# The last two matrix products of a fused attention and SoLU kernel: from a planner's order to an order written out by hand

## The chip, the cores and the metric

The kernel runs on one core of one Trainium2 chip. The metric is the time of one execution on the device in microseconds, and lower is better. A profile of one execution shows five engines: PE (TensorE; PEld is its weight loads), DVE (VectorE), ACT (ScalarE), POOL (GpSimd) and SP (SyncE), whose queue issues nearly all DMA transfers.

## The reference, cut to what matters

Three layers follow each other; the change touches the third only.

```python
def _moe2_ref(x, w_in, w_out, g_ln):          # x: 1792 x 768
    h = x @ w_in                               # 768 x 1024
    h_max = np.max(h, axis=-1, keepdims=True)
    e = np.exp(h - h_max)
    sm = e / (np.sum(e, axis=-1, keepdims=True) + 1e-09)
    solu = h * sm
    mu = np.mean(solu, axis=-1, keepdims=True)
    var = np.mean((solu - mu) ** 2, axis=-1, keepdims=True)
    ln = (solu - mu) / np.sqrt(var + 1e-06) * g_ln
    return (ln @ w_out)                        # 1024 x 768
```

In front of it stand softcapped attention (4 x 12 heads, 448 x 64) and a layer `((x @ w1) * (x @ w2)) @ w3 @ w_out`. The kernel folds `w3 @ w_out @ w_in` into one 1024 x 1024 matrix beforehand, so that `h` is the product of the gated rows `ab` (1792 x 1024) with that matrix.

## The kernel before, in words

**Stages.** Attention (with the folding of weights beside it) and the gated products fill the first 569 us; the change leaves their operations alone. Then come the two stages that it rewrites. Stage 3 computes `h = ab @ folded` and SoLU with the normalisation; stage 4 computes `ln @ w_out` with `g_ln` folded into the weights. Each goes over 7 pairs of 128-row tiles, so there are 14 **rounds**: 0 to 6 in stage 3, 7 to 13 in stage 4.

**One round** is a Strassen-Winograd scheme, function `seven`: seven products named by number, in the order 1, 2, 6, 7, 5, 4, 3, where the plain scheme has eight. A product is 12 matmuls with 512 result columns in stage 3 and 384 in stage 4: four blocks of the inner dimension, times three, since each fp32 operand is split into a high part (a cast to fp32r, ACT, L176) and a low part (a subtraction, DVE, L177). Operands 1, 2 and 4 are quarters of the two tiles; 6, 7, 5 and 3 are sums of quarters (`s1` to `s4`, DVE). Results lie in PSUM banks `u` (two buffers, three products added into one), `y` and `v`. Three are copied out by ACT (L775, the terms p1, u2, p7), three are added to such a copy by DVE (L782, L791, L794), and the last `u` is copied by ACT (L796). A product that adds into `u` or `v` waits for the copy of what stood there.

**SoLU** (`solu`, L824 to L834) of a tile: greatest value of each row (DVE), exp with row sums (ACT), product with `h` (DVE), mean, squares (ACT), variance (DVE, then POOL to the power -1/2), normalisation (DVE), store to a DRAM buffer `c_dr`.

**Stage 4's operands** come back from `c_dr` in 32 x 32 blocks (`load_c`, L865: four DMAs of 128 KB for a tile, in pieces of 128 bytes), are transposed by DVE into PSUM (L839), and split as before. Its weight blocks `wg` (seven, 768 KB each) take the places of stage 3's blocks `ws`: loaded in halves (L518) once the last product with the old block is done, then split by ACT and DVE (L176, L177). Of `ws`, the blocks 4 and 3 (`LATE`) can only be loaded and split during round 0, since their places belong to earlier stages.

**Order.** Nothing in stages 3 and 4 is ordered by hand: a planner that simulates the program's time (`schedule_with_timeline_sim=True`) puts the traced instructions of each engine in order. It may start a product of one round before the products of the round before are done. On the chip each engine then works through its own list in order and waits on semaphores.

Of the kernel before, what the change touches and what calls it, by code (L numbers as in the profile page):

```python
# [9 lines left out]
F32 = mybir.dt.float32  # L10
# [8 lines left out]
P = 128  # L19
# [80 lines left out]
def attention_moe_solu(ctx: ExitStack, tc: tile.TileContext, q, k, v, cap, w12, w3t, wo, win, wout2, g_ln, out):  # L100
# [225 lines left out]
    fw, pos, place, held = {}, [0], {}, {}  # L326
    res = [opened(left, "resa")]
# [43 lines left out]
    def fold():  # L371
# [33 lines left out]
        close(left, 3)  # L405
# [48 lines left out]
    def plan_x(b, parts=range(NPAIR // 2)):  # L454
        for part in parts:
# [6 lines left out]
            def load(i=i, pairs=pairs):  # L462
                rb[i] = conv.tile([P, 2, S], F32, tag="rb", name=f"rb{i}")
# [72 lines left out]
    def plan_last(f):  # L536
        for u in range(2):
            i = len(ahead.items)

            def rest(i=i, u=u):  # L540
                t = conv.tile([P, DM // 2], F32, tag="wg", bufs=2, name=f"wg{f}_{u}")
# [30 lines left out]
    def load_ab(n):  # L572
        for t in (2 * n, 2 * n + 1):
            landing(f"ab{t}", ab_dr[:, :, t * P:(t + 1) * P].rearrange("f p t -> p f t"), NF * P, F32)

    def operand(a, m, x, name, p=None):
        a[m] = op.tile([P, 2, HALF], F32R, tag="op", bufs=NOP, name=f"{name}_{m}") if p is None else p
        split(a[m][:, 0], a[m][:, 1], x)
# [3 lines left out]
    def first_operands():  # L582
        x1, x2 = lands["ab0"], lands["ab1"]
# [3 lines left out]
        def begin(m, x):  # L587
            operand(begun, m, x, "a0", w3p.tile([P, 2, HALF], F32R, tag="w3", bufs=W3, name=f"a0_{m}"))
# [5 lines left out]
    ahead.add("a0", lambda: load_ab(0), lambda: None, first_operands, None, lambda: (NF + 2, PASSES[1][0]) in fin)  # L594
# [168 lines left out]
    NTT = NT // P  # L763
    PAIRS = NTT // 2

    def seven(n, a, wb, w, c1, c2, other):

        def product(bank, m, first):
            for k in range(NF // 2):
                for i, (x, e) in enumerate(THREE):  # L770
                    pe.matmul(bank, a[m][:, x, k * P:(k + 1) * P], wb[m][:, e, k, :], start=(first and k == 0 and i == 0), stop=(k == NF // 2 - 1 and i == 2), skip_group_check=not first)  # L771

        def kept(bank, name):
            t = hp.tile([P, HALF], F32, tag="kept", bufs=2, name=f"{name}_{n}")[:, :w]
            act.copy(t, bank)  # L775
            return t

        u, y, v = (ps.tile([P, HALF], F32, tag=g, bufs=2 if g == "u" else 1, name=f"{g}_{n}")[:, :w] for g in ("u", "y", "v"))
        product(u, 1, True)
        p1 = kept(u, "p1")  # L780
        product(y, 2, True)
        dve.tensor_tensor(c1[:, :w], y, p1, ALU.add)  # L782
        other(0)
        product(u, 6, False)
        u2 = kept(u, "u2")
        other(1)
        product(v, 7, True)
        p7 = kept(v, "p7")
        other(2)
        product(u, 5, False)  # L790
        dve.tensor_tensor(c2[:, w:], u, p7, ALU.add)  # L791
        other(3)
        product(v, 4, False)
        dve.tensor_tensor(c2[:, :w], v, u2, ALU.add)  # L794
        product(u, 3, False)
        act.copy(c1[:, w:], u)  # L796

    def operands(n):

        x1, x2 = (lands.pop(f"ab{t}") for t in (2 * n, 2 * n + 1))  # L800
        a11, a12, a21, a22 = x1[:, :HALF], x1[:, HALF:], x2[:, :HALF], x2[:, HALF:]
        s3, s4 = (hp.tile([P, HALF], F32, tag="sm", bufs=4, name=f"s{i}_{n}") for i in (3, 4))
        a, name = (dict(begun) if n == 0 else {}), f"a{n}"
        if n:
            s1, s2 = (hp.tile([P, HALF], F32, tag="sm", bufs=4, name=f"s{i}_{n}") for i in (1, 2))
            operand(a, 1, a11, name)
            operand(a, 2, a12, name)
            dve.tensor_tensor(s1, a21, a22, ALU.add)
            dve.tensor_tensor(s2, s1, a11, ALU.subtract)
            operand(a, 6, s2, name)  # L810
        else:
            s1, s2 = a.pop("sums")
        dve.tensor_tensor(s3, a11, a21, ALU.subtract)
        operand(a, 7, s3, name)
        operand(a, 5, s1, name)
        operand(a, 4, a22, name)
        dve.tensor_tensor(s4, a12, s2, ALU.subtract)
        operand(a, 3, s4, name)
        return a

    def solu(t, h):
        st = hp.tile([P, 16], F32, tag="st", bufs=3, name=f"st{t}")
        e = hp.tile([P, DF], F32, tag="e", bufs=2, name=f"e{t}")
        dve.tensor_reduce(st[:, 0:1], h, axis=AX.X, op=ALU.max, negate=True)  # L824
        act.activation(e, h, AF.Exp, bias=st[:, 0:1], accum_out=st[:, 1:2])  # L825
        dve.tensor_scalar(st[:, 1:2], st[:, 1:2], 1e-9, None, ALU.add)
        dve.reciprocal(st[:, 2:3], st[:, 1:2])
        dve.scalar_tensor_tensor(e, e, st[:, 2:3], h, ALU.mult, ALU.mult, accum_out=st[:, 3:4])  # L828
        dve.tensor_scalar(st[:, 4:5], st[:, 3:4], -1.0 / DF, None, ALU.mult)
        act.activation(h, e, AF.Square, bias=st[:, 4:5], accum_out=st[:, 5:6])  # L830
        dve.tensor_scalar(st[:, 6:7], st[:, 5:6], 1.0 / DF, 1e-6, ALU.mult, ALU.add)
        pool.tensor_tensor(st[:, 7:8], st[:, 6:7], neghalf, ALU.pow)
        dve.tensor_scalar(e, e, st[:, 4:5], st[:, 7:8], ALU.add, ALU.mult)
        sync.dma_start(out=c_dr[t], in_=e)  # L834

    def turned(n, tps, q):

        tps[q] = ps.tile([P, HALF], F32, tag="tp", bufs=4, name=f"tp{n}_{q}")
        dve.transpose(tps[q], lands[f"c{2 * n + q % 2}"][:, q // 2 * HALF:(q // 2 + 1) * HALF])  # L839

    def turned_operands(n, tps):
        a11, a21, a12, a22 = (tps[q] for q in range(4))
        s1, s2, s3, s4 = (hp.tile([P, HALF], F32, tag="sm", bufs=4, name=f"cs{i}_{n}") for i in range(4))
        a, name = {}, f"c{n}"
        operand(a, 1, a11, name)
        operand(a, 2, a12, name)
        x21 = conv.tile([P, HALF], U32, tag="cv", bufs=2, name=f"x21_{n}").bitcast(F32)
        act.copy(x21, a21)
        dve.tensor_tensor(s1, a22, x21, ALU.add)
        dve.tensor_tensor(s2, s1, a11, ALU.subtract)  # L850
        operand(a, 6, s2, name)
        dve.tensor_tensor(s3, a11, x21, ALU.subtract)
        operand(a, 7, s3, name)
        operand(a, 5, s1, name)
        operand(a, 4, a22, name)
        dve.tensor_tensor(s4, a12, s2, ALU.subtract)
        operand(a, 3, s4, name)
        return a

    def load_c(n):  # L860
        for t in (2 * n, 2 * n + 1):
            lands[f"c{t}"] = conv.tile([P, 2 * HALF], U32, tag="ld", bufs=LANDS, name=f"ldc{t}").bitcast(F32)
            blocks = c_dr[t].rearrange("(i a) (k g b) -> g a k i b", i=P // SQ, g=P // SQ, b=SQ)
            for g in range(P // SQ):
                sync.dma_start(out=lands[f"c{t}"][g * SQ:(g + 1) * SQ].rearrange("p (k i b) -> p k i b", k=NF, b=SQ), in_=blocks[g])  # L865

    w, wg = DM // 2, {}

    def load_wg(m):
        wg[m] = (wsp if m in EARLY[:4] else place["w5"] if m in EARLY else wsl).tile([P, 2, NF // 2, HALF], F32R, tag=f"w{m}", name=f"wg{m}")[:, :, :, :w]  # L870
        for part in range(2):
            block_load(m, part, G4, tg_dr, wg[m])
        for part in range(2):
            block_split(wg[m], part)

    for m in LATE:
        for part in range(2):
            block_load(m, part, W4, tw_dr, ws[m])
    load_ab(1)
    a = operands(0)  # L880
    for m in LATE:
        for part in range(2):
            block_split(ws[m], part)
    for n in range(PAIRS):
        tps, last = {}, n + 1 == PAIRS
        if last:
            load_c(0)
# [82 lines left out]
```

## Time and profile before

| | us |
|---|---|
| median of 3 runs (822.79 to 824.30) | 823.5 |
| the profiled execution | 821.78 |
| its span on the core | 820.0 |
| PE busy | 802.0 (98%) |
| DVE busy | 603.8 (74%) |
| ACT busy | 477.9 (58%) |

A busy share is a mean over all stages. PE time counts a matmul until its modelled end, so a busy PE can still be a slow one: the granted clock beside it tells whether it ran at its upper (1.00) or lower (0.50) level. The profile numbers the kernel's lines; a line of a helper (L176, L177) serves many places, and the tile names tell them apart.

### The profile page before, as it was taken

Reading aid. Unit: us, or ns where it says so; the run is one execution under the profiler, and the core shown is the slowest. Engines: PE = TensorE matmul, PEld = TensorE weight load, DVE = VectorE, ACT = ScalarE, POOL = GpSimd, SP = SyncE. Lnnn points to the kernel's source line nnn. Section 1 sums busy time; section 2 is a strip of 40 time slices with the busy share of each in tenths; the row PEclk is TensorE's granted clock in tenths of the full one; section 3 lists DMA queues with packets and bytes.
Section 4 is the critical chain, followed back from the end, with each engine's and each line's share of the span. In section 5 each row is a group of like instructions: output and inputs, shape, how many; then the busy total and the mean of one; then the engine's idle time right before and its main releaser. Section 6 shows DMA issues by size and latency. Waiting matters only on the chain. (4 is left out here: it accounts for less than half of the span.)

```text
span 820.0 us, 12057 instructions
## 1 busy us (share of the span) xinstructions
PE 802.0 (98%) x4251; PEld 674.0 (82%) x4251; DVE 603.8 (74%) x1076; ACT 477.9 (58%) x739; POOL 74.8 (9%) x147
## 2 busy tenths in 40 slices
PE   8999999999999999999989999999999999889998
PEld 4657888876777888888869999999888888789997
DVE  5989968788776687789756653332988879999851
ACT  6767868787677777667753311112556555765431
POOL 1110110110311211101111000000000000000000
PEclk9999999999999999999999999999999999889999
DMA  7878645678886345779656999981533349858411
GB/s 232 273 265 271 207 162 147 184 228 269 284 274 221 118 133 199 242 261 298 189 172 185 294 373 399 328 259 57 189 114 118 102 103 215 234 143 185 110 40 77
DMA packets 151292, 167.18 MB, mean 204 GB/s; under 512 B 71232, under 2 KB 124224, under 8 KB 149696
## 3 DMA queue, kind: packets, MB, share of 16 engines
q1 hardware_dynamic: 146240, 155.22, 59.2%
q0 software_dynamic: 4992, 11.19, 5.1%
q8 instruction: 33, 0.54, 0.3%
q14 instruction: 27, 0.22, 0.1%
HBM read 113.25 MB, written 47.53 MB: 196 GB/s over the span
## 5 line engine op out<-in xcount | busy, mean ns | idle before, releaser
L610 PE MATMUL ab<-xs,wt 128*128 128x448 f32 x1152 | 236.8, 362 | 0.4 <-ACT x L308 0.4
L610 PEld LDWEIGHTS ab<-xs,wt 128*128 128x128 f32 x1152 | 215.9, 188 | 17.1 <-ACT x L308 0.8
L259 ACT ACTIVATE sc<-sc,qscale 128x896 f32<-128x896 f32 (+1 forms) x96 | 84.9, 885 | 35.2 <-PE sc L251 26.5
L260 ACT ACTIVATE p<-sc,capt 128x896 f32<-128x896 f32 (+1 forms) x96 | 85.6, 917 | 1.4
L292 PE MATMUL o<-hi,v 128*66 128x448 f32 (+1 forms) x360 | 85.0, 371 | 1.3 <-ACT x L308 1.2
L381 PEld LDWEIGHTS f<-w,w_o 128*128 128x128 f32 x576 | 72.0, 189 | 10.1 <-issue 5.7
L771 PE MATMUL u<-ws,a 128*128 128x512 f32 x336 | 79.6, 390 | 0.0
L381 PE MATMUL f<-w,w_o 128*128 128x256 f32 x576 | 77.7, 287 | 0.9 <-DVE w_o L177 0.9
L275 DVE TENSOR_TENSOR lo<-p,hi 128x896 fp32r<-128x896 f32 x60 | 65.0, 1085 | 13.9 <-ACT hi L271 13.7
L771 PEld LDWEIGHTS u<-ws,a 128*128 128x128 f32 x336 | 63.0, 188 | 13.1
L399 PE MATMUL f<-w_i,w 128*128 128x512 f32 x288 | 70.2, 393 | 1.3 <-ACT w L176 1.0
L771 PE MATMUL u<-wg,c 128*128 128x384 f32 x336 | 64.3, 341 | 3.9 <-ACT h L796 3.9
L399 PEld LDWEIGHTS f<-w_i,w 128*128 128x128 f32 x288 | 53.7, 188 | 14.7 <-ACT w L176 1.4
L771 PEld LDWEIGHTS u<-wg,c 128*128 128x128 f32 x336 | 60.3, 193 | 4.5 <-ACT h L796 4.3
L614 ACT COPY a<-ab 128x448 f32<-128x448 f32 x32 | 17.0, 532 | 77.8 <-PE ab L610 71.9
L292 PEld LDWEIGHTS o<-hi,v 128*66 128x66 f32 (+1 forms) x360 | 39.1, 135 | 26.8 <-issue 8.5
L271 ACT CAST hi<-p 128x896 fp32r<-128x896 f32 x60 | 56.6, 947 | 0.3
L618 DVE TENSOR_TENSOR abs<-ab,a 128x448 f32<-128x448 f32 x32 | 19.9, 620 | 44.7 <-PE ab L610 28.7
L171 DVE SCALAR_TENSOR_TENSOR cv<-ld,cv 128x512 uint32<-128x512 uint32 (+1 forms) x80 | 52.0, 658 | 0.6
L172 DVE SCALAR_TENSOR_TENSOR cv<-ld,cv 128x512 uint32<-128x512 uint32 (+1 forms) x80 | 52.0, 658 | 0.5
L170 DVE TENSOR_SCALAR cv<-ld 128x512 uint32<-128x512 uint32 (+1 forms) x80 | 32.6, 411 | 20.5 <-DMA ld<-in_w 8.5
L309 POOL DMA_DIRECT2D xr<-x x48 | 25.4, 533 | 198.0 <-ACT x L308 190.9
(129 smaller groups left out, 1246.9 us busy)
## 6 DMA issues: line engine op xcount, KB each, us to landing
ld<-in_w SPq DMA_DIRECT2D x24, 512.0 KB, 4.9
w_dr<-wt SPq DMA_DIRECT2D x6, 1536.0 KB, 6.9
wt<-w_dr SPq DMA_DIRECT2D x6, 1536.0 KB, 8.1
ld<-in_w3t SPq DMA_DIRECT2D x16, 512.0 KB, 4.2
ab_dr<-abs SPq DMA_DIRECT2D x32, 224.0 KB, 5.0
ldab<-ab_dr SPq DMA_DIRECT2D x14, 512.0 KB, 3.9
c_dr<-e SPq DMA_DIRECT2D x14, 512.0 KB, 3.5
ldc<-c_dr SPq DMA_DIRECT2D x56, 128.0 KB, 3.3
```

Source lines behind the costliest of these rows:

```text
L170: dve.tensor_scalar(x, hi, 5, 2, ALU.logical_shift_left, ALU.logical_shift_right)
L171: dve.scalar_tensor_tensor(x, hi, 0xC0000000, x, ALU.bitwise_and, ALU.bitwise_or)
L172: dve.scalar_tensor_tensor(x, lo, 29, x, ALU.logical_shift_right, ALU.bitwise_or)
L259: act.activation(sc[:, :w, :S], sc[:, :w, :S], AF.Tanh, scale=qscale)
L260: exp_[n, c] = act.activation(p, sc[:, :w, :S], AF.Exp, scale=capt)
L271: act.copy(hi, p)
L275: dve.tensor_tensor(lo, p, raw(hi), ALU.subtract)
L292: product_.append(pe.matmul(outs[n, j][:v_.shape[-1], :S], v_, t[rows, j if c < 3 else 0], **flags))
L381: pe.matmul(f[:, :QW], lw[:, a], rw[:, e], start=(g == 0 and m == 0), stop=(g == NF - 1 and m == 2))
L399: pe.matmul(f, w34[:, a, c, :], rw[:, e], start=(c == 0 and m == 0), stop=(c == NC - 1 and m == 2))
L610: pe.matmul(pp[f, b, i][:, :S], w[:, u], xs[b, c][:, e], start=(c == 0 and m == 0), stop=(c == NC - 1 and m == 2))
L771: pe.matmul(bank, a[m][:, x, k * P:(k + 1) * P], wb[m][:, e, k, :], start=(first and k == 0 and i == 0), stop=(k == NF // 2 - 1 and i == 2 ...
```

## The change

All of stages 3 and 4 is traced in a `manual_schedule` block: each engine runs its instructions in the order in which they are written. The order is a table of slots `(round, product)`. In each slot the product is issued, then the entries planned for that slot, then the copy or addition that takes its result out of PSUM.

- **Order of products**: strictly 1, 2, 6, 7, 5, 4, 3 in each round.
- **Operands**: the cast of an operand stands a slot (mostly) ahead of its subtraction. Operands 1 and 2 are cast and subtracted in one instruction each (1024 wide), likewise 6 and 7. The two transposes of 512 columns become one of 1024.
- **Maxima**: the three additions that leave PSUM in stage 3 become `tensor_tensor_reduce` with a running maximum, the last copy becomes a DVE `tensor_scalar` with a maximum (ACT keeps it in round 6 and in stage 4); the two row-maximum reductions of a pair go, and two negations of a column come.
- **Normalisation** moves from DVE to ACT (`Identity` with scale and bias), with one more POOL instruction for the bias.
- **Weights of stage 4**: each block is one DMA and one split instead of two, with the cast two or more slots after the load is written.
- **A fourth landing**: tiles read back land in four buffers in turn, not three; `rb` and `wg` of the earlier stages get a pool of their own, `early`, that is free in the last two stages. Operand and sum tiles are laid out anew.
- **SoLU of round 6** runs in rounds 9 to 11; before, it was traced in round 7.

```diff
-NOP = 9
+ORDER = EARLY + LATE
+LEAST = -3.0e38
...
+    early = opened(left, "early")
...
+    def product(r, j):
+        m, w = ORDER[j], HALF if r < PAIRS else DM // 2
...
+    def added(r, i, half, g, keep):
+        w = banks[g].shape[-1]
+        dst = h[r][i][:, half * w:(half + 1) * w]
+        if r >= PAIRS:
+            dve.tensor_tensor(dst, banks[g], keeps[keep], ALU.add)
+            return
+        first = (i, half) in ((0, 0), (1, 1))
+        dve.tensor_tensor_reduce(dst, banks[g], keeps[keep], 1.0, LEAST if first else col(r, MAX, i), ALU.add, ALU.max, col(r, MAX if first else MOST, i))
...
+            if r < LAST:
+                dve.tensor_scalar(dst, banks["u"], 0.0, col(r, MAX, 0), ALU.add, ALU.max, accum_out=col(r, MOST, 0))
+            else:
+                act.copy(dst, banks["u"])
...
-        dve.tensor_reduce(st[:, 0:1], h, axis=AX.X, op=ALU.max, negate=True)
+        dve.tensor_scalar(col(r, NEG, i), col(r, MOST, i), -1.0, None, ALU.mult)
...
-        dve.tensor_scalar(e, e, st[:, 4:5], st[:, 7:8], ALU.add, ALU.mult)
+        act.activation(h[r][i], es[r, i], AF.Identity, bias=col(r, SHIFT, i), scale=col(r, RSTD, i))
...
+    def landed():
+        k = taken[0]
+        taken[0] += 1
+        if k % 4 < LANDS:
+            return conv.tile([P, 2 * HALF], U32, tag="ld", bufs=LANDS, name=f"ldx{k}").bitcast(F32)
+        return op.tile([P, 2 * HALF], F32, tag="lx", name=f"ldx{k}")
...
+    plan(0, 0, (load_late, 4), (load_late, 3), (load, 1, 0), (load, 1, 1), (begun_sums,))
+    plan(0, 1, (high, 0, 7))
+    plan(0, 2, (high, 0, 5), (low, 0, 7), (high_w, ws, 4, 0))
+    plan(0, 3, (high, 0, 4), (sum4, 0), (low, 0, 5), (low_w, ws, 4, 0), (high_w, ws, 4, 1))
+    plan(0, 4, (high, 0, 3), (low, 0, 4), (low_w, ws, 4, 1), (high_w, ws, 3, 0), (high_w, ws, 3, 1))
+    plan(0, 5, (low, 0, 3), (low_w, ws, 3, 0), (low_w, ws, 3, 1))
...
+    plan(LAST, 0, (load, A + 1, 0))
+    for m, s in zip(ORDER, range(len(ORDER))):
+        plan(LAST + (s + 1) // 7, (s + 1) % 7, (load_wg, m))
+        if m == 7:
+            plan(LAST, 4, (load, A + 1, 1))
+    for n, s in ((2, 1), (3, 7), (4, 13), (5, 19)):
+        plan(A + s // 7, s % 7, (load, A + n, 0), (load, A + n, 1))
...
+    for m, s, t in ((1, 3, 4), (2, 4, 5), (6, 5, 6), (7, 6, 7), (5, 8, 9), (4, 9, 10), (3, 10, 11)):
+        plan(LAST + s // 7, s % 7, (high_w, wg, m))
+        plan(LAST + t // 7, t % 7, (low_w, wg, m))
...
+    for n in range(PAIRS - 1):
+        plan(A + n + 1, 0, (give, A + n, 1))
+        plan(A + n + 1, 1, (give, A + n, 0))
+    with tc.manual_schedule():
+        for r in range(2 * PAIRS):
+            for j in range(len(ORDER)):
+                product(r, j)
+                for todo in side.pop((r, j), ()):
+                    todo()
+                evict(r, j)
+        for i in (1, 0):
+            give(2 * PAIRS - 1, i)
```

Here `LAST` is 6 and `A` is 7; `high` is a cast on ACT, `low` its subtraction on DVE, `high_w` and `low_w` the same for a weight block, `give` the store of a result tile. The other rounds are planned in the same way: in stage 3 the operands of round n are made from slot -7 to slot 2 counted from its start, in stage 4 from slot -6 to slot 4; the SoLU of round r runs through the slots of round r + 1 (exp in slots 0 and 1, squares in 2 and 3, normalisation in 4 and 5).

## Rows read from the trace of the kernel before

**Rows 1.** Windows: us; busy PE, PEld, DVE, ACT, POOL; granted clock; DMA share; GB/s.

```profile
645.41:664.45 19.04, 19.04 (x85) 15.77 (x85) 15.56 (x30) 10.77 (x19) 1.51 (x3) 1.00 0.43 116
683.49:709.40 25.91, 25.91 (x122) 22.13 (x121) 25.46 (x44) 18.09 (x32) 1.10 (x2) 1.00 0.97 243
709.40:727.83 18.43, 12.04 (x49) 11.71 (x49) 18.43 (x32) 11.72 (x20) 1.10 (x2) 0.75 0.67 168
```

**Rows 2.** Timeline of PE, and of all engines at the end: start, us, instruction, idle.

```profile
569.25 2.96 PE L771 MATMUL u<-ws,a 128*128 128x512 f32 x12
...
629.37 5.60 PE L771 MATMUL u<-ws,a 128*128 128x512 f32 x24
634.81 2.88 PE L771 MATMUL v<-ws,a 128*128 128x512 f32 x12
...
713.35 4.21 PE L771 MATMUL u<-wg,c 128*128 128x384 f32 x12 [3.94 <-ACT h L796]
...
724.74 3.61 PE L771 MATMUL y<-wg,c 128*128 128x384 f32 x12 [2.45 <-DVE o L782]
...
736.83 4.32 PE L771 MATMUL u<-wg,c 128*128 128x384 f32 x24
740.99 1.55 PE L771 MATMUL y<-wg,c 128*128 128x384 f32 x8
...
816.07 0.48 ACT L796 COPY o<-u 128x384 f32<-128x384 f32 x1 [5.76 <-PE u L771]
```

**Rows 3.** Timeline of the SP queue and of ACT where the stages meet.

```profile
682.44 6.65 SPq L865 DMA_DIRECT2D ldc<-c_dr  x7
...
701.33 5.00 SPq L865 DMA_DIRECT2D ldc<-c_dr  x5
...
708.39 2.10 SPq L518 DMA_DIRECT2D wg<-tg_dr  x2
...
710.59 0.83 ACT L176 CAST wg<-wg 128x768 fp32r<-128x768 f32 x1 [3.17 <-DMA wg<-tg_dr]
...
712.72 0.58 ACT L796 COPY h<-u 128x512 f32<-128x512 f32 x1
```

**Rows 4.** Groups by line and shape, 600 to 820 us: busy us, mean ns.

```profile
L177 DVE TENSOR_TENSOR c<-cs,c 128x512 fp32r<-128x512 f32 x28 | 18.8, 683 | 4.5 <-ACT c L176 4.1
L828 DVE SCALAR_TENSOR_TENSOR e<-e,st,h 128x1024 f32<-128x1024 f32 x14 | 17.8, 1278 | 0.0
L176 ACT CAST c<-cs 128x512 fp32r<-128x512 f32 x28 | 17.0, 622 | 8.9 <-PE u L771 8.1 <-PE v L771 0.8
L825 ACT ACTIVATE e<-h,st 128x1024 f32<-128x1024 f32 x13 | 15.0, 1153 | 7.4 <-DMA c_dr<-e 3.4 <-issue 3.2 <-DVE st L824 0.8
L824 DVE TENSOR_REDUCE st<-h 128x1 f32<-128x1024 f32 x12 | 14.1, 1208 | 1.9 <-ACT h L796 1.9
L177 DVE TENSOR_TENSOR wg<-wg 128x768 fp32r<-128x768 f32 x14 | 13.2, 946 | 0.5 <-ACT wg L176 0.5
L176 ACT CAST wg<-wg 128x768 fp32r<-128x768 f32 x14 | 11.5, 835 | 9.7 <-DMA wg<-tg_dr 5.0 <-DMA wg<-wg_dr 4.6
L833 DVE TENSOR_SCALAR e<-e,st 128x1024 f32<-128x1024 f32 x14 | 11.2, 802 | 2.0 <-POOL st L832 1.9
L791 DVE TENSOR_TENSOR h<-u,p 128x512 f32<-128x512 f32 x6 | 4.1, 685 | 0.2 <-PE u L771 0.2
```

**Rows 5.** DMA issues, whole execution: count, KB each, median us to landing.

```profile
ldc<-c_dr SPq DMA_DIRECT2D x56, 128.0 KB, 3.3
out<-o SPq DMA_DIRECT2D x14, 384.0 KB, 2.3
ws<-w_dr SPq DMA_DIRECT2D x6, 512.0 KB, 8.9
wg<-tg_dr SPq DMA_DIRECT2D x8, 384.0 KB, 5.7
```

**Rows 6.** Timeline of DVE in round 0: two subtractions end to end.

```profile
577.06 1.29 DVE L177 TENSOR_TENSOR a<-s,a 128x512 fp32r<-128x512 f32 x2
```

More of the change, by code (lines that the diff above doesn't have):

```diff
@@ L570, in attention_moe_solu, with gated_tile, load_first @@
         plan_block(EARLY[4], part)
[L572 to L578, printed above, removed]
+    def gated_tile(t):
+        return ab_dr[:, :, t * P:(t + 1) * P].rearrange("f p t -> p f t")
+    def load_first():
+        for t in range(2):
+            landing(f"x{t}", gated_tile(t), NF * P, F32)
     begun = {}
     def first_operands():
-        x1, x2 = lands["ab0"], lands["ab1"]
+        x1, x2 = lands["x0"], lands["x1"]
         s1, s2 = first_sums = [conv.tile([P, HALF], U32, tag="cv", bufs=2, name=f"s{i}_0").bitcast(F32) for i in (1, 2)]
@@ L762, in attention_moe_solu @@
     ps = ps_cm.__enter__()
[L763 to L796, printed above, removed]
@@ L836, in turned @@
[L836 to L858, printed above, removed]
@@ L860, in load_c @@
[L860 to L874, printed above, removed]
@@ L876, in attention_moe_solu @@
-    for m in LATE:
+    PAIRS = NT // P // 2
+    LAST = PAIRS - 1
+    wg, banks, keeps, h, a, x, sums, es, sts = {}, {}, {}, {}, {0: begun}, {0: (lands.pop("x0"), lands.pop("x1"))}, {0: {}}, {}, {}
+    MAX, MOST, NEG, SUM, INV, TOTAL, MEAN, SQUARES, VAR, RSTD, SHIFT = range(0, 22, 2)
+    side, both, taken = {}, {}, [2]
+    def product(r, j):
+        m, w = ORDER[j], HALF if r < PAIRS else DM // 2
+        g, first = {1: "u", 2: "y", 6: "u", 7: "v", 5: "u", 4: "v", 3: "u"}[m], m in (1, 2, 7)
+        if first:
+            banks[g] = ps.tile([P, HALF], F32, tag=g, bufs=2 if g == "u" else 1, name=f"{g}_{r}")[:, :w]
+        b = ws if r < PAIRS else wg
+        for k in range(NF // 2):
+            for i, (p, e) in enumerate(THREE):
+                pe.matmul(banks[g], a[r][m][:, p, k * P:(k + 1) * P], b[m][:, e, k, :], start=(first and k == 0 and i == 0), stop=(k == NF // 2 - 1 and i == 2), skip_group_check=not first)
@@ new lines, in store, with load @@
+    def store(r, i):
+        sync.dma_start(out=c_dr[2 * r + i], in_=h[r][i])
+    def landed():
[4 more added lines that the diff above has]
+        return op.tile([P, 2 * HALF], F32, tag="lx", name=f"ldx{k}")
+    def load(r, i):
+        x.setdefault(r, {})[i] = t = landed()
+        if r < PAIRS:
+            sync.dma_start(out=t.rearrange("p (f t) -> p f t", t=P), in_=gated_tile(2 * r + i))
+            return
+        blocks = c_dr[2 * (r - PAIRS) + i].rearrange("(i a) (k g b) -> g a k i b", i=P // SQ, g=P // SQ, b=SQ)
+        for g in range(P // SQ):
+            sync.dma_start(out=t[g * SQ:(g + 1) * SQ].rearrange("p (k i b) -> p k i b", k=NF, b=SQ), in_=blocks[g])
@@ new lines, in high @@
+    def high(r, m):
+        if m in (1, 6, 7):
+            t = op.tile([P, 2, 2, HALF], F32R, tag="two", bufs=3, name=f"a{r}_{m}")
+            if m != 7:
+                a.setdefault(r, {}).update({m: t[:, 0], m + 1: t[:, 1]})
+                both[r, m] = t[:, :, 0], t[:, :, 1]
+            else:
+                a[r][m] = t[:, 1]
+                both[r, m] = t[:, 1, 0], t[:, 1, 1]
+        else:
+            a[r][m] = t = op.tile([P, 2, HALF], F32R, tag="one", bufs=3, name=f"a{r}_{m}")
+            both[r, m] = t[:, 0], t[:, 1]
+        act.copy(both[r, m][0], source(r, m))
@@ new lines, in parts, with high_w, low_w, plan @@
+    def parts(t, part):
+        return (t[:, i, rows(part), :] for i in range(2))
+    def high_w(t, m, part=None):
+        hi, lo = parts(t[m], part)
+        act.copy(hi, raw(lo))
+    def low_w(t, m, part=None):
+        hi, lo = parts(t[m], part)
+        dve.tensor_tensor(lo, raw(lo), raw(hi), ALU.subtract)
+    def plan(r, j, *entries):
+        for f, *args in entries:
+            side.setdefault((r, j), []).append(lambda f=f, args=args: f(*args))
+    A = PAIRS
+    STEPS = ((turn, 0), (turn, 1), (high, 1), (low, 1), (copy21,), (sum1,), (sum2,), (sum3,), (high, 6), (low, 6), (high, 5), (low, 5), (high, 4), (low, 4), (sum4,), (high, 3), (low, 3))
@@ new lines, in attention_moe_solu, with give @@
+    plan(A + 2, 2, (greatest, LAST), (negate, LAST, 0), (negate, LAST, 1))
+    for i in range(2):
+        plan(A + 2, 3 + i, (exponential, LAST, i))
+        plan(A + 3 + i, 0, (weigh, LAST, i))
+        plan(A + 3 + i, 1, (squares, LAST, i))
+        plan(A + 3 + i, 3, (spread, LAST, i))
+        plan(A + 3 + i, 4, (normal, LAST, i))
+        plan(A + 3 + i, 5, (store, LAST, i))
+    def give(r, i):
+        t = 2 * (r - A) + i
+        sync.dma_start(out=out[t * P:(t + 1) * P, :], in_=h[r][i])
```

207 lines of the change are left out of this document (129 added, 78 removed).

## The prediction

> **What bounds the kernel now.** I read the busy windows first, then PE's timeline, then what PE waited for. In a steady round of stage 3 the windows show PE without a gap at the upper clock level, DVE busy 15.56 of 19.04 us and ACT 10.77 [rows 1]. So PE bounds the stage, and nothing done for DVE or ACT there is worth time. Where the stages meet it is different: from 709.40 to 727.83 PE is busy 12.04 of 18.43 us and its granted clock is 0.75 on average, that is, part of the stretch at the lower level [rows 1].
>
> How much is that in all? Stage 3 begins at 569.25 and the last product ends where the last copy starts, at 816.07 [rows 2]: 246.8 us. At PE's steady pace 24 matmuls take 634.81 - 629.37 = 5.44 us in stage 3 (227 ns each) and 740.99 - 736.83 = 4.16 us in stage 4 (173 ns) [rows 2]. Each stage has 7 x 84 = 588 matmuls, so at that pace they take 133.3 + 101.9 = 235.2 us. **The excess is 11.6 us**, and this is all that an order can win here. Of it 3.94 + 2.45 = 6.4 us are two waits; most of the rest is slow work behind them (the product at 713.35 took 4.21 us for 12 matmuls, where 2.08 is the pace) [rows 2].
>
> What is late there? PE waited 3.94 us for an ACT copy out of `u`. That copy ran at 712.72, and before it ACT stood 3.17 us at a cast of a `wg` block whose load had not landed [rows 3]. SP had issued that block's load behind tiles read back from `c_dr` (7 issues from 682.44, 5 more from 701.33), and was still issuing `wg` at 708.39 [rows 3], while the DMA engines were 0.97 busy [rows 1]. So loads in an unlucky order stopped ACT, and ACT's list held back a copy that had nothing to do with them. The second wait, for DVE's addition to `y`, comes from the DVE backlog: DVE is busy 25.46 of 25.91 us up to 709.40 and all 18.43 us after it [rows 1].
>
> The Trainium skill, TensorE: Matmul & The Clock Gate, Part 1 (Architectural detail), says that ScalarE and VectorE take their queue strictly first in, first out. The trace agrees (the copy behind the cast, 3.17 us). By this rule any late load or column in the new order stops all that is written behind it, which speaks against the change; the row alone says that it cost 3.94 us once. The last rival below takes the rule at its worst.
>
> **The change part by part.** Prices are means of [rows 4].
>
> *Stage 3, DVE.* Two maxima go (2 x 1.21 = 2.42 us a round) and two normalisations (2 x 0.80 = 1.60). Seven subtractions of 0.683 become two wide and three narrow: 512 columns take 0.683 and 768 take 0.946, so 1024 take about 1.21, and 2 x 1.21 + 3 x 0.683 = 4.47 replaces 4.78. Four results are now taken with a maximum. No row shows that instruction: it can't well be cheaper than the plain addition (0.685), and the nearest row with a second result, L828, takes 1.28 for twice the columns. I take 0.8, close to the addition, since the width and the streams are the same; 0.685 and 1.28 are the bounds. That is 4 x 0.8 - 3 x 0.685 = +1.15. Two negations of one column are the only other addition. DVE comes to 15.56 - 2.42 - 1.60 - 0.31 + 1.15 = 12.4 us of 19.04.
>
> *Stage 3, ACT.* Two normalisations come (priced like the exp, 1.15 each), one copy goes (0.58), the casts fall from 7 x 0.622 to about 2 x 1.05 + 3 x 0.622: 10.77 + 2.31 - 0.58 - 0.39 = 12.1 us. Both lists fit with a third to spare, so the steady rounds cost and win **nothing**: PE's own 19.04 us hides them.
>
> *Round 0 and 1.* DVE and ACT also split the two late `ws` blocks here. The loads of these blocks cannot all be issued before the last product of stage 2 ends, and such a load takes up to 8.9 us to land [rows 5]. ACT reaches the first cast in the third slot, some 6.5 us into the round; the u2 copy stands behind it and PE needs it at 4 x 2.72 = 10.9. Landing 8 to 9.5, the wide cast 1.05 and the copy 0.58 make 9.6 to 11.1: a wait of 0 to 0.3. Second, three of round 0's operands still lie in memory of an earlier stage over which the new operand tiles may be laid; if the cast of operand 7 has to wait until product 6 is done, PE stands for a cast and a subtraction, 0.62 + 0.68 = 1.3. I take half of it, 0.6. DVE's list for slots 5 and 6 of round 0 sums to 8 us against 5.4, so it enters round 1 some 2.6 us late (3.8 at the price of 1.28) and works this off by slot 4; what PE needs of it has one slot of slack, 2.72. I take 0.1.
>
> *The meeting of the stages.* The weight loads now start one per slot from the end of product 1 of round 6, one DMA each; each waits on SP for its product, with the read-backs and the SoLU stores of round 5 queued behind it, which nobody needs within a round. The first two tiles of stage 4 are read a round earlier, and only two more stand among the weights. Each cast stands two slots behind its load, 5.4 us; the halves took 5.7 us to land in a full queue [rows 5]. ACT's list in round 6: four weight casts (0.835 + 3 x 0.213 = 1.47 for 1536 columns) 5.9, six activations 6.9, four operand casts 2.9, four copies 2.3: **18.0 us of 19.04**. Instructions end to end overlap a little (two subtractions in 1.29 rather than 1.37 us, [rows 6]), so it is rather 17. ACT ends the round 2 to 2.5 us late, with the p1 copy of round 7 due one slot of 2.08 us after its product. So about 1 us of lateness is free, and then each us costs PE one. DVE carries a similar backlog through slots 0 to 4 of round 7 (a weight subtraction of about 1.7 in each slot of 2.08). I take 0.7 for both, bounds 0 and 4.
>
> *Stage 4.* SoLU of round 6 is spread over three rounds of 14.6 us, and DVE never has more than 14.5 in one. One new wait: a result tile has one buffer per half, so the addition of product 2 in a round waits until the stores of the round before have landed, and on SP these are written behind eight read-back issues. Round 8: the second transpose of round 7 frees a landing at about 13.6 us from round 7's start, four issues at 0.95 (6.65/7, [rows 3]) end at 17.4, two store issues and 2.3 to land [rows 5] make 20.5. Behind that addition DVE has the subtraction of operand 5, done at 20.5 + 0.55 + 0.68 = 21.7; PE needs it at 14.56 + 8.32 = 22.9. Slack 1.2, so 0.3 for four such rounds.
>
> *The rest.* The earlier stages keep their operations; the tail behind the last copy keeps its copy and its two stores. A steady pace from the first matmul on is not reached (loads run beside round 0): 0.2.
>
> **The sum.** 11.6 - (0.1 + 0.6 + 0.1 + 0.7 + 0.3 + 0.2) = 11.6 - 2.0 = **9.6 us**. The profiled execution took 821.78 (span 820.0 and 1.8 around it), so the same execution would take 812.2; it lies 1.7 under the median of 823.5, and the median becomes **813.9**.
>
> **The rivals.**
>
> *Half of it comes back as waits* (0.20). If the maximum costs 1.28, DVE enters round 1 and round 7 1.2 us later each, and both have next to no slack left: about 2 us. If the weight loads land 3 us late, ACT holds PE for 2. With the operand wait in full (1.3 instead of 0.6) that is up to 5 more: 816.5 to 821. For it speaks how little slack rounds 1, 6 and 7 have; against it, that no single one of these is likely to be at its bound.
>
> *The loads stay the bound where the stages meet* (0.08). From the start of round 6 to the last weight cast, 19.04 + 3 x 2.08 = 25.3 us, the queue must move 7 x 0.79 MB of weights, two tiles of 0.52 and two stores of 0.52: 7.6 MB. At the 243 GB/s that the window to 709.40 shows at a share of 0.97 [rows 1] this takes 31 us, 6 too many; with the lower clock behind such a wait, as before, 9 to 10 us are gone and the time is 822 to 824. Against it: twelve issues of the window's mix were read-backs in small pieces [rows 3], now eight.
>
> *The maximum is a slow instruction* (0.06), on the other side. It stands three times in every round of stage 3 in front of a bank. DVE's 12.4 us hold 2.4 for these three; it becomes the bound when one takes (19.04 - 10.0)/3 = 3.0 us, and the whole gain is gone at 3.0 + 9.6/(3 x 7) = 3.5. At 4 us, 21 us are lost, 11 more than the gain: 835. Nothing in the rows comes near 3 us; it is open only because the instruction is not among them.
>
> *A list that stops in every round* (0.05). Strictly ordered lists replace a planner's. If in each of 13 rounds ACT's copies of p1, u2 or p7 came 1.5 us too late (behind exp or squares that wait for DVE's columns), that is 20 us: 830. Each such pair stands a slot apart in the table, which speaks against it.
>
> **How the numbers follow.** My forecast, 811 to 816.5, has 0.61; half back 0.20; loads 0.08; the two slow cases 0.11. About 0.2% (1.6 us) is what a measurement can tell here. Below 821.9 lie the first two: 0.81. Within 0.2% lies most of the load case: 0.06; slower 0.13. The range for 8 in 10 takes the first two cases, 811 to 820.5.
>
> **What would show it.** Right: PE without waits above 1 us between 569 and 816 (counted from the same start), clock 1.00 throughout the meeting of the stages, the span shorter by 8 to 11 us, all of it in that stretch; DVE near 12 to 13 us a steady round, `tensor_tensor_reduce` at 0.7 to 0.9. Wrong: PE waits in rounds 0 or 1 on ACT's cast of operand 7 or a `ws` cast; ACT idle for a `wg` load with PE behind it; DVE without idle time in rounds 2 to 5; or a stage 3 that starts at another time than 569.25, which would be the planner's doing in the stages that I hold unchanged.

## The result and the profile after

| | before | after |
|---|---|---|
| median of four runs each, taken side by side, us | 823.88 (822.79 to 824.30) | 814.88 (813.38 to 815.99) |
| ratio, 95% interval | | 0.9887 [0.9868, 0.9907] |
| profiled execution, us | 821.78 | 815.22 (span 813.4) |
| first product of stage 3 starts, us | 569.25 [rows 2] | 570.79 |
| copy of the last product starts, us | 816.07 [rows 2] | 809.46 |
| the stretch between the two, us | 246.8 | 238.7 |

Faster by 9.0 us in the median; 813.9 was forecast. The two profiled executions differ by 6.6 only, because the changed one reached stage 3 1.5 us later. Up to that point the instruction lists differ in one load only (a 512 KB tile that SP issues at 542.31 us before and inside stage 3 after), and the two executions stand 1.6 us apart long ahead of it: the same attention matmul starts at 97.14 and at 98.76. So this 1.5 is not the change's doing. From here on I read **the stretch**: 8.1 us shorter, with 3.5 left above the 235.2 of PE's pace. (The expectations below say 238.5 for it: they end it with the last product at its pace, 807.17 + 2.08.)

The windows of the changed kernel; columns as in [rows 1], which show the same three places before, to within 1.5 us:

```profile
645.00:664.04 19.04, 19.04 (x86) 15.78 (x85) 13.01 (x31) 12.47 (x18) 2.34 (x4) 1.00 0.33 110
683.00:709.00 26.00, 26.00 (x122) 22.23 (x121) 22.14 (x40) 20.02 (x27) 2.55 (x4) 1.00 0.88 229
709.00:727.83 18.83, 17.24 (x97) 16.34 (x96) 15.43 (x19) 9.61 (x12) 0.00 (x0) 1.00 0.91 216
```

The steady round is PE's 19.04 us as before, with DVE at 13.0 (15.6 before) and ACT at 12.5 (10.8): 2.5 us less on DVE, with nothing to show for it. The gain is in the third line. PE is busy 17.24 of 18.83 us where it was 12.04 of 18.43, and the granted clock is 1.00, where it was 0.75.

What is left of waiting, from the timeline of PE (the last line is ACT's, from the timeline of all engines at the end):

```profile
570.79 2.96 PE L782 MATMUL u<-ws,a 128*128 128x512 f32 x12
...
587.38 3.35 PE L782 MATMUL u<-ws,a 128*128 128x512 f32 x14
591.01 2.56 PE L782 MATMUL u<-ws,a 128*128 128x512 f32 x10 [0.28 <-DVE a L910]
...
714.09 2.35 PE L782 MATMUL u<-wg,a 128*128 128x384 f32 x12 [0.65 <-ACT u L786]
717.38 2.35 PE L782 MATMUL v<-wg,a 128*128 128x384 f32 x12 [0.93 <-ACT p L786]
...
809.46 0.48 ACT L830 COPY o<-u 128x384 f32<-128x384 f32 x1 [5.76 <-PE u L782]
```

Three waits, 1.86 us in all, where before there were two of 6.4 [rows 2] and a fallen clock behind them. Where the two at the meeting of the stages come from is seen on SP's queue and on ACT:

```profile
697.62 4.98 SPq L879 DMA_DIRECT2D ldx<-c_dr  x4
702.70 1.94 SPq L523 DMA_DIRECT2D wg<-tg_dr  x2
704.74 0.57 SPq L862 DMA_DIRECT2D c_dr<-h  x1
705.40 1.06 SPq L523 DMA_DIRECT2D wg<-wg_dr  x1
...
709.39 1.48 ACT L954 CAST wg<-wg 128x1536 fp32r<-128x1536 f32 x1 [1.62 <-DMA wg<-tg_dr]
712.19 1.49 ACT L954 CAST wg<-wg 128x1536 fp32r<-128x1536 f32 x1 [1.31 <-DMA wg<-tg_dr]
713.57 0.47 ACT L786 COPY u<-u 128x384 f32<-128x384 f32 x1
715.48 1.47 ACT L954 CAST wg<-wg 128x1536 fp32r<-128x1536 f32 x1 [1.44 <-DMA wg<-wg_dr]
716.86 0.47 ACT L786 COPY p<-v 128x384 f32<-128x384 f32 x1
```

It is the picture of [rows 3] once more, smaller. Four read-back issues hold SP for 4.98 us, the weight blocks written behind them go out from 702.70 on, ACT stands three times at a cast (1.62, 1.31, 1.44 us), and behind the second and the third stands a copy that PE needs.

The prices, by line and shape, 600 to 813 us; columns as in [rows 4]:

```profile
L859 ACT ACTIVATE h<-e,st 128x1024 f32<-128x1024 f32 x14 | 17.4, 1246 | 1.8 <-POOL st L856 1.8
L910 DVE TENSOR_TENSOR a<-s,a 128x1024 fp32r<-128x1024 f32 x12 | 14.7, 1224 | 4.5 <-ACT a L906 4.5
L958 DVE TENSOR_TENSOR wg<-wg 128x1536 fp32r<-128x1536 f32 x7 | 12.3, 1753 | 2.4 <-ACT wg L954 2.4
L954 ACT CAST wg<-wg 128x1536 fp32r<-128x1536 f32 x7 | 10.4, 1486 | 4.4 <-DMA wg<-tg_dr 2.9 <-DMA wg<-wg_dr 1.4
L808 DVE CUSTOM_DVE_ANT_0 h<-v,u,st 128x512 f32<-128x512 f32 x6 | 4.5, 750 | 3.9 <-PE v L782 3.9
L808 DVE CUSTOM_DVE_ANT_0 h<-u,p 128x512 f32<-128x512 f32 x6 | 4.2, 692 | 9.7 <-ACT h L859 7.5 <-ACT a L906 1.7 <-PE u L782 0.4
L828 DVE TENSOR_SCALAR_CACHE_REDUCE h<-u,st 128x512 f32<-128x512 f32 x5 | 3.8, 751 | 2.9 <-PE u L782 2.8
```

The addition with a maximum (L808) takes 0.69 to 0.75 us, next to the plain addition's 0.685 [rows 4].

### The profile page after: what moved, and what is told of

Read it like the earlier page. It is cut to its first block, busy times and chain, and to the rows that moved or that the text cites. A ratio compares the mean times of both kernels' runs of the same rounds, so it can differ in the third digit from the quotient of the medians.

```text
span 813.4 us, 11974 instructions
## 1 busy us (share of the span) xinstructions
PE 799.6 (98%) x4251; PEld 672.0 (83%) x4251; DVE 585.0 (72%) x1050; ACT 487.7 (60%) x714; POOL 80.5 (10%) x161
## 4 chain that ended last, share of the span: by engine, by line
PE 69%; DMA 12%; DVE 11%; ACT 4%; issue 3%; SPq 1%; POOL 0%; DVEq 0%; ACTq 0%; POOLq 0%
PE ab L615 21%; PE u L782 14%; PE v L782 7%; PE o L293 7%; PE f L401 6%; PE f L383 5%; PE y L782 4%; PE sc L252 3%; DVE cv L172 2%; DVE cv L173 2%; DMA ld<-in_w 2%; DMA rb<-r_dr 1%; DVE cv L171 1%; DMA wg<-wg_dr 1%; DMA inv<-x 1%
## 5 line engine op out<-in xcount | busy, mean ns | idle before, releaser
L782 PE MATMUL u<-wg,a 128*128 128x384 f32 x336 | 62.2, 335 | 0.7 <-ACT u L786 0.7
L782 PEld LDWEIGHTS u<-wg,a 128*128 128x128 f32 x336 | 58.5, 188 | 1.3 <-ACT u L786 1.0
L906 ACT CAST a<-s 128x512 fp32r<-128x512 f32 (+1 forms) x42 | 31.3, 755 | 31.2 <-DVE s L928 16.9
```

The lines of the kernel that those rows point to most:

```text
L782: pe.matmul(banks[g], a[r][m][:, p, k * P:(k + 1) * P], b[m][:, e, k, :], start=(first and k == 0 and i == 0), stop=(k == NF // 2 - 1 and ...
```

## The experiments

The first question was whether the order gives the gain or the cheaper work in it. Every kernel was timed in five rounds beside the kernel before, and its ratio is its time over that kernel's. The kernel before took 825.2 to 825.5 us there and 823.88 beside the changed kernel, so ratios, not medians, are to be compared across the two. All edits lie behind the start of stage 3. Each stretch is that of one profiled execution; how far it varies between executions of one kernel was not measured.

### Order or work

**e1, the new work in the planner's order.**
```diff
-    with tc.manual_schedule():
+    with nullcontext():
```


> The changed kernel with all its new operations, but without the order by hand: the planner orders the last two stages. Theory O (the order gives the gain: it puts the weight loads and casts where the stages meet so that PE does not wait): most of the 9 us come back, 819 to 826, with PE waits of several us and a lower granted clock between 700 and 735. Theory W (the gain is less work on DVE and ACT, whoever orders it): 814.5 to 816.5.

Measured: 823.27, ratio 0.9976 [0.9954, 0.9999]; stretch 245.8. In the stretch the work alone gives 1.0 of 8.1 us, by the ratio about a fifth of the gain. The wait is only another one, as PE's timeline shows:

```profile
732.59 6.00 PE L782 MATMUL u<-wg,a 128*128 128x384 f32 x24 [4.67 <-DVE st L845]
```

**e2, the kernel before with the maxima in the evictions and the normalisation on ACT**, in the planner's order. (The last copy of a round goes to DVE here too, and the normalised tile is stored from `h`.)
```diff
-        dve.tensor_tensor(c1[:, :w], y, p1, ALU.add)
+        added(c1[:, :w], y, p1, 0, True)
...
-        dve.tensor_reduce(st[:, 0:1], h, axis=AX.X, op=ALU.max, negate=True)
+        dve.tensor_scalar(st[:, 0:1], st[:, 9:10], -1.0, None, ALU.mult)
...
-        dve.tensor_scalar(e, e, st[:, 4:5], st[:, 7:8], ALU.add, ALU.mult)
+        act.activation(h, e, AF.Identity, bias=st[:, 10:11], scale=st[:, 7:8])
```


> The kernel before, in its planner's order, with the maxima taken in the evictions and the normalisation on ACT. Theory O: 821.5 to 824.5, since the steady rounds hide DVE anyway and the waits where the stages meet stay. Theory W: 815 to 818.

Measured: 830.77, ratio 1.0068 [1.0046, 1.0090]; stretch 252.9. Both expectations missed. With less work on DVE (588.1 us busy in the whole execution, 603.8 before) it is *slower*: the planner now lets PE wait 8.81 us at the place of [rows 2]'s second wait, and the product behind takes 4.21 us:

```profile
730.50 4.21 PE L779 MATMUL y<-wg,c 128*128 128x384 f32 x12 [8.81 <-DVE o L772]
```

**e3, the written order with separate maxima** (and the last copy on ACT).
```diff
-        dve.tensor_tensor_reduce(dst, banks[g], keeps[keep], 1.0, ..., ALU.add, ALU.max, ...)
+        dve.tensor_tensor(dst, banks[g], keeps[keep], ALU.add)
...
-        dve.tensor_scalar(col(r, NEG, i), col(r, MOST, i), -1.0, None, ALU.mult)
+        dve.tensor_reduce(col(r, NEG, i), h[r][i], axis=AX.X, op=ALU.max, negate=True)
```


> The changed kernel with the row maxima as separate reductions again (plain additions out of PSUM, two reductions of 1024 columns a pair, the last copy on ACT), in the same order by hand. It adds 2.42 + 3 x 0.685 - 4 x 0.80 = 1.3 us of DVE a steady round. Theory O: 814.5 to 816.5, hidden in the steady rounds, up to 1 us more in round 1, which enters with a backlog. Theory W: 818 or more.

Measured: 816.15, ratio 0.9890 [0.9857, 0.9922]; stretch 238.3. The maxima in the evictions are worth nothing that shows.

**e11, the written order with the normalisation back on DVE.**
```diff
-        act.activation(h[r][i], es[r, i], AF.Identity, bias=col(r, SHIFT, i), scale=col(r, RSTD, i))
+        dve.tensor_scalar(h[r][i], es[r, i], col(r, MEAN, i), col(r, RSTD, i), ALU.add, ALU.mult)
```


> The written order with the normalisation back on VectorE as in the kernel before (one instruction of about 1.1 us on VectorE in place of 1.25 us on ScalarE and 0.3 us on GpSimd). Theory that in a written order such work is hidden on either engine: stretch 238 to 239, ratio 0.988 to 0.990. Rival, that VectorE, the fuller of the two, delays the evictions by it: stretch 239.5 to 243, with TensorE waits on VectorE of over 1 us.

Measured: 817.11, ratio 0.9914 [0.9880, 0.9947]; stretch 239.3, between the two expectations. PE's waits stand at the places of the changed kernel's three (0.3, 1.0 and 0.9 us; 0.3, 0.7 and 0.9 there), none of them a new one on DVE. The instruction took 0.81 us there, as in the kernel before, and not the 1.1 expected. The ratio lies beyond the range that was expected, but its interval takes in 0.9887, so nothing is shown lost or won.

### Which engines' order

**e5, only SP's list as written.**
```diff
-    with tc.manual_schedule():
+    with tc.manual_schedule(engines={mybir.EngineType.SP}):
```


> The changed kernel with only SP's list ordered by hand in the last two stages; PE, ACT, DVE and POOL are the planner's, as in e1. Theory L (the loads where the stages meet are what the written order puts right): ratio 0.988 to 0.991, the stretch from the start of stage 3 to the last product 238 to 240 us, as in the changed kernel (238.5). Theory C (the lists of ACT and DVE are what it puts right): ratio 0.995 to 1.000, the stretch 244 to 247 us, as in e1 (245.8).

**e6, only ACT's, DVE's and POOL's lists as written**, the column engines' (the same line with `Activation, DVE, Pool`).

> The changed kernel with the lists of ACT, DVE and POOL ordered by hand, those of PE and SP by the planner. Theory C: ratio 0.988 to 0.991 and a stretch of 237 to 240 us. Theory L: ratio 0.995 to 1.000, 243 us or more, with ACT idle at casts of weight blocks whose loads are late.

**e9, these three and SP**, with the planner's order on PE alone (the same line).

> Written order on SyncE, VectorE, ScalarE and GpSimd, the planner's on TensorE alone. The loads alone gave a stretch (first product of stage 3 to the start of the last product's copy) of 242.5 us, the column engines alone 247.6, all engines 238.5, the kernel before 246.8. Theory that TensorE's list is only the products in their rounds, which the planner finds too once operands come on time: stretch 238 to 239.5, ratio 0.988 to 0.990. Rival, that the planner's place for products and transposes costs by itself: stretch 241 to 245 with a wait of TensorE's over 2 us that stands behind an instruction whose operand is late while others are ready.

**e10, SP and PE** (the same line).

> Written order on SyncE and TensorE, the planner's on the three engines between them. Theory that the casts' and evictions' order matters: ScalarE and VectorE hold copies and splits behind work that waits, TensorE waits 2 us or more in the stretch, which is 241 to 245 us, ratio 0.993 to 0.998. Rival, that weights in time and the products in order are enough: 238 to 239.5, ratio 0.988 to 0.990.

| lists as written | median, us | ratio [95%] | stretch, us |
|---|---|---|---|
| none (e1) | 823.27 | 0.9976 [0.9954, 0.9999] | 245.8 |
| ACT, DVE, POOL (e6) | 826.57 | 1.0025 [1.0001, 1.0048] | 247.6 |
| SP (e5) | 822.75 | 0.9965 [0.9939, 0.9990] | 242.5 |
| SP, ACT, DVE, POOL (e9) | 821.36 | 0.9958 [0.9935, 0.9981] | 246.5 |
| SP, PE (e10) | 820.30 | 0.9941 [0.9915, 0.9967] | 242.0 |
| all (the changed kernel) | 814.88 | 0.9887 [0.9868, 0.9907] | 238.7 |

None of the four parts tried carries the gain. With SP's list in it, a part gives 0.4 to 0.6% of the 1.1%, and ACT, DVE and POOL without SP give nothing: in e6 ACT stood 5.4 us at weights that SP's planned list brought late. I had expected 238 to 240 of e5 and missed. (Ten of its twelve runs took 821.9 to 824.8 us and two 817; the profiled one is one of the two, so its stretch may flatter it.) In e10 the theory came out: waits of 4.4 us in all behind ACT's copies. PE's list alone, and PE's with the three column engines' (ACT, DVE, POOL), were not tried.

In e9 the lists of SP and of the column engines are those of the changed kernel, and the rival came out, with a stretch of 246.5 beyond its range (the ratio shows a gain of about 3.5 us, the profiled execution 0.3, so this execution was not a typical one). PE had a wait of 2.51 us, and then paid a clock at the lower level. Its timeline of PE, and windows around it (columns as in [rows 1]):

```profile
717.67 3.21 PE L782 MATMUL u<-wg,a 128*128 128x384 f32 x12 [2.51 <-ACT u L786]
```
```profile
714.00:717.60 3.60, 1.16 (x7) 0.84 (x5) 2.09 (x2) 2.53 (x3) 0.00 (x0) 1.00 1.05 404
717.60:721.00 3.40, 3.26 (x13) 2.75 (x13) 1.88 (x2) 1.97 (x4) 0.00 (x0) 0.70 1.04 294
721.00:724.00 3.00, 2.78 (x8) 2.38 (x9) 3.00 (x4) 0.83 (x2) 0.00 (x0) 0.50 0.95 151
```

From 717.67 to 726.35 PE ran 28 matmuls in 8.7 us, where the pace is 28 x 0.173 = 4.8. In stage 4 it waited three times more, 0.57 us each, for ACT's copy of `u`; the changed kernel has no such wait there. The first wait shows how the lists hang together. A weight block is loaded when PE is done with the old one, so PE's order decides when SP may go on. In e9 SP stood up to 5.0 us for one product, in the changed kernel up to 2.3, and its queue reads

```profile
697.51 1.64 SPq L523 DMA_DIRECT2D wg<-tg_dr  x2
699.23 8.08 SPq L879 DMA_DIRECT2D ldx<-c_dr  x4
707.41 1.30 SPq L523 DMA_DIRECT2D wg<-tg_dr  x2
708.81 0.57 SPq L862 DMA_DIRECT2D c_dr<-h  x1
709.47 0.51 SPq L523 DMA_DIRECT2D wg<-wg_dr  x1
```

The last three blocks go out from 707.41 on, 136.1 us after the start of stage 3 (571.31); in the changed kernel, with the same list, it is 131.9 (702.70 - 570.79). ACT stood 4.9 us at late weights in e9, 4.4 in the changed kernel, and the copy of `u` that PE waited for came at 145.8 us, there at 142.8 (713.57 - 570.79).

### The loads at the meeting of the stages

**e4, the second read-back of round 8 behind the weight loads.**
```diff
+    plan(A, 0, (load, A + 1, 1))
...
-        if m == 7:
-            plan(LAST, 4, (load, A + 1, 1))
```


> The changed kernel with one read-back moved on SP: the second tile of stage 4's second pair is loaded after the last weight block, not between blocks 7 and 5. In the changed kernel those four issues take SP from 697.6 to 702.6, and ACT then stands 1.6, 1.3 and 1.4 us at the casts of blocks 5, 4 and 3 with PE waiting 0.7 and 0.9 behind it. Theory O (the order of the issues on SP makes these waits): ACT's three waits under 0.5 us together, 812.3 to 813.6. Rival Q (the DMA queue is full there whatever its order): the waits stay, 814.0 to 815.8.

Measured: 814.83, ratio 0.9863 [0.9835, 0.9891]; stretch 236.3. SP's queue and ACT in it:

```profile
696.27 8.68 SPq L523 DMA_DIRECT2D wg<-tg_dr  x4
...
707.15 0.37 SPq L523 DMA_DIRECT2D wg<-wg_dr  x1
707.61 6.55 SPq L879 DMA_DIRECT2D ldx<-c_dr  x4
...
709.69 2.87 ACT L954 CAST wg<-wg 128x1536 fp32r<-128x1536 f32 x2
713.42 0.48 ACT L786 COPY u<-u 128x384 f32<-128x384 f32 x1 [0.86 <-PE u L782]
```

Two casts run back to back, the copy of `u` now waits for PE and not PE for it, and both waits at the meeting are gone: 2.4 us of stretch for four issues moved behind the weights. So it was these four in front, not a queue too full for the weights. e8 below has the same order on SP and no such wait either, with a stretch of 235.8; the changed kernel, e3 and e11, with the four in front, have 238.3 to 239.3. The median does not tell: it lies in the range of rival Q, but by the ratio (0.9863 x 823.88 = 812.6) in that of theory O, and the intervals of e4 and of the changed kernel overlap.

How the four make the weights late is told by the issues and landings of the last three blocks, in us after the first product of stage 3:

| block | issued, changed kernel | issued, e4 | landed, changed kernel | landed, e4 |
|---|---|---|---|---|
| 5 | 131.9 | 128.9 | 138.6 | 134.5 |
| 4 | 133.0 | 131.6 | 141.4 | 137.3 |
| 3 | 134.6 | 134.3 | 144.7 | 141.0 |

All three land some 4 us later. For block 5 most of it, 3.0 us, is SP standing at the four issues. Blocks 4 and 3, whose casts hold the copies that PE needs, are issued only 1.4 and 0.3 us later; the rest is a longer way from issue to landing (8.4 and 10.1 us, where e4 has 5.7 and 6.7), behind the bytes of the tile.

**e7, each weight load a slot later.**
```diff
-        plan(LAST + (s + 1) // 7, (s + 1) % 7, (load_wg, m))
+        plan(LAST + (s + 2) // 7, (s + 2) % 7, (load_wg, m))
```


> The changed kernel with each of the seven weight loads written one slot later (2.72 us in stage 3, 2.08 in stage 4), the casts where they were. By the prediction about 1 us of lateness is free and then each us costs PE one. Theory L: ACT waits at the casts of all blocks, 8 us or more together, and the stretch grows from 238.5 to 240 to 244 us. Rival (the casts have slack enough, the full queue decides when blocks land): 238 to 239 us.

Measured: 819.53, ratio 0.9927 [0.9902, 0.9952]; stretch 239.9. A slot of 2.72 us costs 1.2 of stretch, just under the 240 to 244 expected; PE's waits there are 1.7 and 1.1, and ACT stood 5.7 us at the casts of three blocks, where 8 or more at all of them were expected. By the ratio it lost more, 0.4% or 3.3 us (the two intervals just touch), which the one profiled execution (815.25, the lowest of twelve) does not show.

**e8, e4 and one sum of round 1 a slot later**, to take the 0.28 us out of round 1.
```diff
-    operands(1, None, None, -2, -1, None, -2, -1, -1, -1,
+    operands(1, None, None, -2, -1, None, -1, -1, -1, -1,
```


> e4 with one addition of round 1 (s1) moved on DVE behind the subtraction that round 1's first product waits for. In e4 that product stands 0.3 us for it with some 0.3 us of slow restart, and this is the only wait left. Expected: no wait of PE left from the start of stage 3 to the end, the stretch 235.5 to 236.0 us (236.2 in e4), the ratio 0.985 to 0.988. If the wait has another cause behind it (DVE's list as a whole), it stays at 236.2.

Measured: 815.10, ratio 0.9883 [0.9851, 0.9915]; stretch 235.8 (573.07 to 808.91), without any wait of PE, 0.6 above the pace. No version has a shorter stretch. That it beats the changed kernel in time is not shown: 815.10, 814.83 and 814.88 are one number here.

**e12, the kernel before with its weight loads at high priority.**
```diff
-            load_wg(1)
-            a = turned_operands(0, tps)
-            for m in (EARLY + LATE)[1:]:
-                load_wg(m)
+            with tc.high_priority():
+                for m in EARLY + LATE:
+                    load_wg(m)
+            a = turned_operands(0, tps)
```


> The kernel before with the eight landings of the left side's weights put ahead of everything else that the planner may issue, nothing else changed; the order of all engines stays the planner's. Theory that lateness of these loads is a matter of priority and can be had without a written order: ScalarE's waits for landed weights vanish, stretch 241 to 244 us as with the loads alone in written order, ratio 0.993 to 0.998. Rival, that landings early in the list hold SyncE's queue while their tiles are still in use, and the loads behind them come late: stretch 246 to 255, ratio 1.0 to 1.01.

Measured: 827.24, ratio 1.0027 [1.0008, 1.0046]; stretch 248.5. It answers another question than the one asked: SP's list kept its order, and all that moved, by the names in the trace, is one weight cast on ACT and one weight subtraction on DVE, each ahead of one neighbour. In this execution the two waits of [rows 2] are not 3.94 and 2.45 but

```profile
716.29 2.35 PE L771 MATMUL u<-wg,c 128*128 128x384 f32 x12 [3.25 <-ACT h L796]
...
728.56 3.91 PE L771 MATMUL y<-wg,c 128*128 128x384 f32 x12 [5.75 <-DVE o L782]
```

The two swaps did not make all of this. The weight cast that stands ahead of both waited longer already, in the kernel before and here:

```profile
694.85 0.84 ACT L176 CAST wg<-wg 128x768 fp32r<-128x768 f32 x1 [3.90 <-DMA wg<-wg_dr]
```
```profile
698.57 0.83 ACT L176 CAST wg<-wg 128x768 fp32r<-128x768 f32 x1 [5.19 <-DMA wg<-wg_dr]
```

Counted from the start of stage 3 it ran at 125.6 and at 127.2 us, for a load that SP issued at 121.0 and 121.3. So nearly the same lists differ by 1.7 us in the stretch of one execution, and part of that is how long loads take to land. Whether the planner could be brought to issue the weights first was not tried further.

## Why the prediction was right, and where its terms were not

**Where the gain lies: right.** The excess of 11.6 us over the pace was all there was to win, the steady rounds gave nothing, and the changed kernel is left with 3.5. e3 and e11 agree with the first step: DVE's or ACT's work is hidden in a written order. e1 and e2 show that without the order the new work pays little (0.2%), and that a part of it can cost.

**The six terms**, predicted and then measured in the stretch:

| term | predicted | measured | from |
|---|---|---|---|
| late `ws` block before the u2 copy | 0.1 | 0 | no such wait |
| cast of operand 7 in older memory | 0.6 | 0 | no such wait |
| DVE late into round 1 | 0.1 | 0.5 | 587.38 + 14 x 0.227 = 590.56, next start 591.01; gone in e8 |
| meeting of the stages | 0.7 | 2.2 | below |
| result tile in stage 4 | 0.3 | 0.2 | another cause |
| start of stage 3 | 0.2 | 0.3 | four products at 2.80 instead of 2.72 |
| sum | 2.0 | 3.2 | of the 3.5 left |

*The meeting* was mis-sized. The mechanism was the one named (ACT stands at a cast whose load is late, a copy behind it holds PE), the size is 0.65 + 0.93 of waits and 0.6 of slower restarts behind them. What I missed was the step before. I set two slots, 5.4 us, between a load and its cast, against 5.7 us to land. Blocks 5, 4 and 3 landed 6.7, 8.4 and 10.1 us after their issue, and SP issued them up to 3.0 us later than without the four read-backs in front, which held it for 4.98 us. I had the tile in a sum of bytes for the whole round, and not as what stands ahead of three blocks. ACT's own list was not the limit: it was busy 15.4 us in round 6 (685.89 to 704.93), where I had 17 to 18. The Trainium skill, TensorE: Matmul & The Clock Gate, Part 1 (Architectural detail), has the rule that the queues of ScalarE and VectorE run strictly first in, first out; the trace agrees, with the 1.44 us at the cast of 715.48 in front of the copy that PE waited 0.93 for.

*The result tile* was misread. The two results of rounds 8, 10 and 12 lie in buffers named `h1`, those of 7, 9, 11 and 13 in `o`; they alternate, so the wait that I priced from one buffer does not exist. The 0.2 us at 725.81 (2.32 for a product of 2.08) is a wait for a subtraction (0.27 at the weight load of 726.27, for DVE's subtraction of operands 6 and 7). That the numbers are near each other is chance.

*Operand 7* was an unknown priced in the middle; the cast did not stop. *The maximum* was taken at 0.8 and measured 0.69 to 0.75 and 0.08 for reading it out.

**How much of it was luck.** 813.9 lies within 1.0 of 814.88 partly by chance. What is left above the pace is 3.5 us and not 2.0. In the forecast, 0.7 was priced for two waits that never came, against 1.5 too little at the meeting and 0.4 in round 1; and the median fell 0.9 us more than the stretch.

**The signs.** Of those named for being right, four came: no wait of PE above 1 us (0.93 at most), a clock of 1.00 through the meeting, DVE at 13.0 us in a steady round, the maximum near its price. The span is shorter by 6.6 us and not by 8 to 11, since stage 3 began later. Two signs of being wrong came as well: ACT idle for a `wg` load with PE behind it, which is the mis-sized term, and a start of stage 3 other than 569.25, which is spread between executions and not the planner's doing.

**The rivals.** Half of the gain coming back as waits: one of its three parts came, weights some 4 us late (against e4), and PE paid 2.2 for it; the maximum and operand 7 cost nothing. (Two times of the rivals do not follow from their own sums: 5 us above 813.9 is 818.9 and not 821, and 20 above it is 834 and not 830.) The loads as the bound: refuted by e4, where the same bytes, in another order, make no wait. Its 243 GB/s was no ceiling: the window from 714.00 in e9 moved 404. A slow maximum: no. A list that stops in every round: PE has no wait between 593 and 714 us. In e9, where only PE's list was the planner's, something like it did come up, three times 0.57 us.

**What is open.** The median gained 9.0 us and the stretch 8.1. The 0.9 between them is within the spread of the stages before, as is the order of e4, e8 and the changed kernel. The order was never tried with the old work as a whole: e3 and e11 take out the maxima and the normalisation, but the wide casts and subtractions, the weight loads in one piece and the fourth landing stood in every written order. That the order is needed for the gain is shown; that it would be enough without these three is not.

## What to carry to other kernels

When one engine runs at its pace in the steady rounds, sum its excess over that pace and see where it lies; here 11.6 us at one seam were the whole prize, and taking 2.5 us a round off the second engine was worth nothing. Here a written order paid as a whole: lists of some engines by hand and of others by a planner gave half of it or less in the four parts tried, since, as in e9, one engine's order decides when another may go on. In such an order ask of each urgent load what stands *ahead of it in its queue*, in issue time and in bytes: a tile of 512 KB that nobody needed yet cost 2.4 us of the stretch here, and moving it behind was one line.

## What the runs showed of the hardware that I had not expected

- **The same lists at different speed.** Over the fourteen profiled executions stage 3 begins between 568.80 us (e5) and 575.97 us (e6), with the same instructions ahead of it, but for one load. e4's 2.4 us of stretch do not show in its median. The stretch leaves this spread out, but has one of its own: the medians of e5, e7 and e9 do not go with the stretch of their one profiled execution, and e12's differs from that of the kernel before by 1.7 with nearly the same lists.
- **Clock after a wait.** Waits of 0.65 and 0.93 us left the granted clock at 1.00, and so did one of 3.25 us in e12 (12 matmuls in 2.35 us behind it, window 1.00). One of 2.51 us in e9 was followed by 0.70 and 0.50, that is 1.2 GHz, for several us. The length of a wait alone does not tell what follows it.
- **A maximum for next to nothing.** An addition from PSUM with a running maximum took 0.69 to 0.75 us on 512 columns, with 0.08 to read it out; the separate maximum on 1024 columns took 1.21 [rows 4].
